# Softplus by one ScalarE activation function in a fused attention and MLP kernel

## The chip, the cores and the metric

One Trainium2 chip, one of its cores. The metric is the device time of one execution in microseconds (us). The kernel before has a median of 710.45 us over three runs (707.38 to 711.43).

The engines go by the names of the profile: PE is TensorE (matmuls) and PEld its weight loads, DVE is VectorE, ACT is ScalarE, POOL is GpSimd, SP is the engine whose queue issues the transfers. Each engine runs its own instructions in a fixed order and waits where a result of another engine is missing.

## What is computed

Eight batches of eight heads. Attention runs both ways between 512 rows of `x` and 32 rows of `state` per head; the 544 result rows of a batch then go through a two-layer network with softplus between the layers (4,352 rows, 512 to 2048 to 512).

```python
scores = scale * x @ state.T;  a = softmax(scores);  xread = a @ state
scores2 = scale * state @ x.T; a2 = softmax(scores2); sread = a2 @ x
rows = concat([xread, sread])          # per batch: 512 + 32 rows, heads side by side
h = rows @ w_in
g = np.maximum(h, 0.0) + np.log1p(np.exp(-np.abs(h)))
out = g @ w_out
```

## The kernel before

All operands are float32. For the large products every operand is split into a high part, rounded to the type `fp32r` (line 90 on ACT, or line 83 on POOL), and a low part, the remainder (line 91 on DVE or POOL); a product is then three passes: high by high, low by high, high by low. The attention result and the first layer are merged: `state @ w_in` is formed once for the heads (tiles `Vf`, split into `vhl`), so the hidden layer of a batch is attention weights `aT` times `vhl`.

The unit of work is one hidden tile of 128 features by 512 rows. `gemm1` (line 478) writes it into a PSUM bank `h`, of which there are two. `softplus` (lines 460 to 469) turns it into `ghi` and `glo`, of which there are three each, and `gemm2` (line 485) multiplies them into four accumulators `acc`. Each bank `h` is given back when the last instruction that reads it is done: line 465 on DVE, which reads it for the maximum. There are 136 such tiles, 16 for each of the eight batches and 8 for the `sread` rows of all batches (line 525 in place of line 478). A queue `pend` puts `gemm2` of a tile about three tiles behind its `gemm1`.

Strings of letters set the program order: `|` is a `gemm1` with its softplus, `g` a `gemm2`, `p` the split of a piece of `vhl`, `F` a fetch, `W` the preparation of a tile of `w_out`, `v`, `V`, `U` pieces of `state @ w_in`, and `a`, `b`, `c` the next step of the attention of a batch. `START` runs while the weights arrive, then `BLOCK2`, `BLOCK3` and `BLOCK` for the batches 2 to 6, then the `sread` tiles and `LAST`. From this program order the framework makes the order of each engine, by dependences and its own durations.

What else ACT does matters here. In `START` it converts the 64-bit weights (`as_f32`, line 111, an activation called Prelu), copies `state @ w_in` out of PSUM (lines 165, 172, 207, 216) and saves partial sums (line 574). Through all batches it makes the softmax exponentials (line 361 for `a`, line 380 for `a2`: `e2`, which PE transposes at line 392), copies PSUM (lines 240, 351, 395, 422), and rounds high parts (line 90). ACT evaluates functions from a table that holds one set of functions; line 50 loads the set `natural_log_exp_and_others` once at the start, and the instruction that does it is ACT_TABLE_LOAD. The program is compiled with such a load wherever a function is called that the loaded set lacks.

Of the kernel before, what the change touches and what calls it, by code (L numbers as in the profile page):

```python
# [13 lines left out]
AF = mybir.ActivationFunctionType  # L14
ALU = mybir.AluOpType
# [32 lines left out]
def attention_then_softplus_mlp(ctx: ExitStack, tc, xn, xt, zq, zp, stk, w_in, w_out, out):  # L48
    nc = tc.nc
# [8 lines left out]
    def sb(tag, shape, dt=F32, bufs=1):  # L58
        uid[0] += 1
        return sp.tile(shape, dt, tag=tag, name=f"{tag}_{uid[0]}", bufs=bufs)  # L60
# [25 lines left out]
    def split(hi, lo, src, *what):  # L86
        if ("hi",) + what in MOVED:
            pool_copy(hi, src)
        else:
            nc.scalar.copy(hi, src)  # L90
        vec(*what).tensor_tensor(lo, src, f32(hi), ALU.subtract)  # L91
# [367 lines left out]

    def softplus(h, *what):  # L460
        t = sb("t", [P, 512], bufs=2)
        nc.scalar.activation(t, h, AF.Abs)  # L462
        nc.scalar.activation(t, t, AF.Exp, scale=-1.0)  # L463
        nc.scalar.activation(t, t, AF.Ln, bias=1.0)  # L464
        nc.vector.scalar_tensor_tensor(t, h, 0.0, t, ALU.max, ALU.add)  # L465
        ghi = sb("ghi", [P, 512], F32R, bufs=3)
        glo = sb("glo", [P, 512], F32R, bufs=3)
        split(ghi, glo, t, "g", *what)
        return ghi, glo

    def gemm1(b, ft):
        h = bank("h", 2)
        n = 0
        cs = slice(P * (ft % 2), P * (ft % 2) + P)
        assert made["aT", b] == 2
        for g in range(2):
            for vi, ai in PASSES:
                nc.tensor.matmul(h, Vhl[b, ft // 2][:, vi, g, cs], aT[b][:, ai, g], start=(n == 0), stop=(n == 5))  # L478
                n += 1
        return softplus(h, min(b, 4), ft)  # L480
# [37 lines left out]
    def gemm1_read(u):  # L518
        assert made["read"] == B
        h = bank("h", 2)  # L520
        for i in range(2):
            n = 0
            for kt in range(4):
                for wi, si in PASSES:
                    nc.tensor.matmul(h[:, 256 * i:256 * i + 256], Whl[u, i][:, wi, kt, :], sreadT[:, si, kt, :],  # L525
                                     start=(n == 0), stop=(n == 11))
                    n += 1
        return softplus(h, B, u)
# [186 lines left out]
```

## Time and profile before

| | before |
|---|---|
| median of three runs | 710.45 us |
| profiled execution, its own time | 708.3 us |
| its span, first to last instruction | 706.3 us |
| PE busy | 680.7 us (96%) |
| ACT busy | 501.3 us (71%) |
| DVE busy | 466.3 us (66%) |
| POOL busy | 172.8 us (24%) |
| mean granted TensorE clock | 0.995 |

The span is told from the first to the last instruction; 2.0 us of the profiled execution's time lie around it. "Busy" is the share of time in which an engine has an instruction in execution. An instruction of ACT starts before the one ahead of it is quite finished, when it doesn't depend on it, so the distance between two starts is a little shorter than the duration of one. A wait is told by the engine that stood still, the line it stood at and the instruction that ended the wait. A granted clock of 1.00 is TensorE's upper level (2.4 GHz), 0.50 its lower one (1.2 GHz).

### The profile page before, as it was taken

To read this page: it belongs to the slowest core of one execution; us is meant where nothing else is said; L and a number is where in the kernel's file an instruction comes from. 1 tells how busy PE (TensorE), PEld (TensorE's weight loads), DVE (VectorE), ACT (ScalarE), POOL (GpSimd) and SP (SyncE) were. 2 spreads that over 40 slices of the span, in tenths; PEclk is the share of its full clock that TensorE was granted. 3 is DMA by queue.
4 is the path that set the end of the run, shared out by engine and by line. 5 is a ranking of instruction groups with operands and counts; after the bars stand their busy time and mean duration, and the time that the engine had idled before them with its cause. 6 is when DMAs were issued, how large, how long until landed. Compare 5 with 4: busy or idle time off the path is not lost.

```text
span 706.3 us, 9196 instructions
## 1 busy us (share of the span) xinstructions
PE 680.7 (96%) x3012; PEld 536.0 (76%) x3012; DVE 466.3 (66%) x818; ACT 501.3 (71%) x914; POOL 172.8 (24%) x170
## 2 busy tenths in 40 slices
PE   5679999999999999999999999999999999999997
PEld 2455666888877878778777887888788888888876
DVE  4499768936798997796858754875487534544322
ACT  2588988766588778799878856875687556657452
POOL 1221102665233565201201070107010510000220
PEclk9999999999999999999999999999999999999999
DMA  8768896221335456354433311320111013412001
GB/s 267 239 246 287 265 306 199 74 61 48 96 104 164 149 162 204 105 198 153 132 92 108 103 52 38 104 75 14 47 60 59 5 58 104 143 52 60 1 0 59
DMA packets 42063, 82.91 MB, mean 117 GB/s; under 512 B 6176, under 2 KB 13088, under 8 KB 42016
## 3 DMA queue, kind: packets, MB, share of 16 engines
q1 hardware_dynamic: 42016, 82.33, 36.3%
q8 instruction: 23, 0.38, 0.2%
q14 instruction: 24, 0.20, 0.1%
HBM read 56.62 MB, written 25.69 MB: 117 GB/s over the span
## 4 chain that ended last, share of the span: by engine, by line
PE 81%; ACT 9%; DVE 7%; issue 2%; DMA 1%; POOL 0%; SPq 0%; ACTq 0%; DVEq 0%; POOLq 0%
PE acc L485 47%; PE h L478 22%; PE h L525 3%; PE aux L235 2%; PE aux L411 1%; ACT t L463 1%; ACT t L462 1%; ACT t L464 1%; ACT ghi L90 1%; PE aux L341 1%; PE aux L347 1%; DVE k L91 1%; PE aux L392 1%; DMA xT<-in_xt_dram 1%; PE aux L200 1%
## 5 line engine op out<-in xcount | busy, mean ns | idle before, releaser
L485 PE MATMUL acc<-wout,ghi 128*128 128x512 f32 x1088 | 343.1, 394 | 0.9 <-DVE StK L577 0.5
L485 PEld LDWEIGHTS acc<-wout,ghi 128*128 128x128 f32 x1088 | 203.2, 188 | 48.2 <-issue 2.4
L485 PE MATMUL acc<-wout,glo 128*128 128x512 f32 x544 | 214.1, 394 | 0.0
L478 PE MATMUL h<-aT,vhl 128*128 128x512 f32 x768 | 203.7, 402 | 4.3 <-DVE t L465 3.8
L478 PEld LDWEIGHTS h<-aT,vhl 128*128 128x128 f32 x768 | 142.2, 189 | 44.4 <-DVE t L465 9.6
L465 DVE SCALAR_TENSOR_TENSOR t<-h,t 128x512 f32<-128x512 f32 x136 | 93.1, 686 | 97.4 <-ACT t L464 97.1
L462 ACT ACTIVATE t<-h 128x512 f32<-128x512 f32 x136 | 81.4, 598 | 77.4 <-DVE glo L91 37.7
L485 PEld LDWEIGHTS acc<-wout,glo 128*128 128x128 f32 x544 | 102.1, 188 | 22.7 <-issue 0.7
L91 DVE TENSOR_TENSOR glo<-t,ghi 128x512 fp32r<-128x512 f32 x100 | 70.3, 703 | 35.4 <-ACT ghi L90 14.8
L90 ACT CAST ghi<-t 128x512 fp32r<-128x512 f32 x104 | 64.5, 620 | 36.4 <-PE acc L485 23.2
L464 ACT ACTIVATE t<-t 128x512 f32<-128x512 f32 x136 | 86.2, 634 | 2.8
L463 ACT ACTIVATE t<-t 128x512 f32<-128x512 f32 x136 | 86.3, 634 | 2.2
L91 DVE TENSOR_TENSOR vhl<-vf,vhl 128x512 fp32r<-128x512 f32 x62 | 47.1, 760 | 36.0 <-ACT vhl L90 34.0
L83 POOL TENSOR_SCALAR ghi<-t 128x512 fp32r<-128x512 f32 x32 | 21.7, 679 | 180.7 <-PE acc L485 139.8
L91 POOL TENSOR_TENSOR glo<-t,ghi 128x512 fp32r<-128x512 f32 x36 | 48.5, 1351 | 49.6 <-ACT ghi L90 43.1
L90 ACT CAST vhl<-vf 128x512 fp32r<-128x512 f32 x59 | 36.4, 616 | 18.1 <-PE h L525 11.7
L368 POOL TENSOR_TENSOR T<-T,sm 128x512 f32<-128x512 f32 x13 | 15.1, 1160 | 120.7 <-DVE sm L367 92.3
L111 ACT ACTIVATE k<-k 128x512 f32<-128x512 f32 (+1 forms) x32 | 20.2, 645 | 10.3 <-DMA k<-in_w_in_dram 7.7
L525 PEld LDWEIGHTS h<-sreadT,vhl 128*128 128x128 f32 x192 | 23.6, 191 | 2.4 <-DVE t L465 2.2
L525 PE MATMUL h<-sreadT,vhl 128*128 128x256 f32 x192 | 24.9, 286 | 0.1
L352 DVE TENSOR_TENSOR k<-aux,k 64x512 f32<-64x512 f32 x24 | 16.4, 682 | 12.5 <-ACT k L351 12.3
L115 DVE SCALAR_TENSOR_TENSOR wt<-k,wt 128x512 int32<-128x512 int32 (+1 forms) x26 | 20.2, 791 | 2.0 <-ACT k L111 1.7
(161 smaller groups left out, 697.6 us busy)
## 6 DMA issues: line engine op xcount, KB each, us to landing
vd<-ve SPq DMA_DIRECT2D x44, 256.0 KB, 3.0
xT<-in_xt_dram SPq DMA_DIRECT2D x16, 512.0 KB, 4.1
x<-in_xn_dram SPq DMA_DIRECT2D x16, 512.0 KB, 3.8
k<-in_w_out_dram SPq DMA_DIRECT2D x16, 512.0 KB, 4.8
vf<-vd SPq DMA_DIRECT2D x64, 128.0 KB, 2.6
k<-in_w_in_dram SPq DMA_DIRECT2D x12, 512.0 KB, 4.7
out_dram<-o SPq DMA_DIRECT2D x24, 256.0 KB, 2.0
wt<-wsc SPq DMA_DIRECT2D x16, 256.0 KB, 2.9
```

The lines of the kernel that those rows point to most:

```text
L83: nc.gpsimd.tensor_scalar(dst, src, 1.0, 0.0, ALU.mult, ALU.add)
L90: nc.scalar.copy(hi, src)
L91: vec(*what).tensor_tensor(lo, src, f32(hi), ALU.subtract)
L111: nc.scalar.activation(h2, f32(hi), AF.Prelu, scale=2.0 ** -112, alpha=-(2.0 ** 32))
L115: nc.vector.scalar_tensor_tensor(u, h2.bitcast(I32), 3, u, ALU.logical_shift_left, ALU.bitwise_or)
L462: nc.scalar.activation(t, h, AF.Abs)
L463: nc.scalar.activation(t, t, AF.Exp, scale=-1.0)
L464: nc.scalar.activation(t, t, AF.Ln, bias=1.0)
L465: nc.vector.scalar_tensor_tensor(t, h, 0.0, t, ALU.max, ALU.add)
L478: nc.tensor.matmul(h, Vhl[b, ft // 2][:, vi, g, cs], aT[b][:, ai, g], start=(n == 0), stop=(n == 5))
L485: nc.tensor.matmul(acc[c], g[gi][:, c0:c0 + P], wout[ft][:, wi], start=(ft == first and i == 0), stop=(ft == last and i == 2))
L525: nc.tensor.matmul(h[:, 256 * i:256 * i + 256], Whl[u, i][:, wi, kt, :], sreadT[:, si, kt, :], start=(n == 0), stop=(n == 11))
```

## The change

The softplus of a tile is one activation instead of three and a DVE instruction. The reading of `h` on DVE is gone, and with it the four instructions' intermediate values in `t`. Strings, tiles and numbers of buffers stay as they are. Behind the changed lines all line numbers fall by three (line 574 becomes 571).

```diff
     def softplus(h, *what):
         t = sb("t", [P, 512], bufs=2)
-        nc.scalar.activation(t, h, AF.Abs)
-        nc.scalar.activation(t, t, AF.Exp, scale=-1.0)
-        nc.scalar.activation(t, t, AF.Ln, bias=1.0)
-        nc.vector.scalar_tensor_tensor(t, h, 0.0, t, ALU.max, ALU.add)
+        nc.scalar.activation(t, h, AF.Softplus)
         ghi = sb("ghi", [P, 512], F32R, bufs=3)
```

The order of ACT at the first softplus of the program, before. `t` is the softplus tile, `h` its bank, `k` the words of a weight tile (line 111), `T` the softmax of `a`.

```order
L111 ACTIVATE k_69_272<-k_64_261 128x512
L462 ACTIVATE t_364<-h_357 128x512
L90 CAST sreadT<-h_344 64x2x32
L463 ACTIVATE t_364<-t_364 128x512
L464 ACTIVATE t_364<-t_364 128x512
L90 CAST sreadT<-h_344 64x2x32
L361 ACTIVATE T_375<-T_375 128x512
L111 ACTIVATE k_86_321<-k_76_290 128x512
L111 ACTIVATE k_88_328<-o_108 128x256
```

The same place after the change.

```order
L111 ACTIVATE k_69_272<-k_64_261 128x512
L462 ACT_TABLE_LOAD
L462 ACTIVATE t_364<-h_357 128x512
L90 CAST sreadT<-h_344 64x2x32
L90 CAST ghi_366<-t_364 128x512
L111 ACT_TABLE_LOAD
L111 ACTIVATE k_86_321<-k_76_290 128x512
L111 ACTIVATE k_88_328<-o_108 128x256
```

Two activations of `t` are gone, the rounding of `ghi` stands where they stood, and the table is loaded twice: once for the softplus and once for the next weight conversion. The second place is ACT in the attention of a later batch, at the exponential of `a2` (line 380), before.

```order
L462 ACTIVATE t_3610<-h_3603 128x512
L380 ACTIVATE e_890_3704,rs_3705<-k_883_3671,nm_3701 128x512
L463 ACTIVATE t_3610<-t_3610 128x512
L464 ACTIVATE t_3610<-t_3610 128x512
L90 CAST a2T_3720<-aux_3715 128x8x64
L90 CAST ghi_3599<-t_3594 128x512
L361 ACTIVATE T_3723<-T_3723 128x512
L462 ACTIVATE t_3634<-h_3627 128x512
```

The same exponentials after the change.

```order
L380 ACT_TABLE_LOAD
L380 ACTIVATE e_890_3500,rs_3501<-k_883_3467,nm_3497 128x512
L462 ACT_TABLE_LOAD
L462 ACTIVATE t_3415<-h_3408 128x512
L90 CAST ghi_3404<-t_3402 128x512
L90 CAST a2T_3516<-aux_3511 128x8x64
L361 ACT_TABLE_LOAD
L361 ACTIVATE T_3519<-T_3519 128x512
L90 CAST ghi_3417<-t_3415 128x512
L462 ACT_TABLE_LOAD
L462 ACTIVATE t_3436<-h_3429 128x512
```

Four loads stand around the two exponentials; the casts and copies between them need none. In all there are 60 loads in the changed program where one was. Of the 59 new ones 24 stand from the first softplus to the last weight conversion, all in `START`, one before the softplus that follows it, and 34 in the rest, before exponentials of the attention and the softplus behind them. The order on PE and DVE is shifted by a few places in `START` too, since the framework places instructions by when it takes their inputs to be there.

## Rows read from the trace of the kernel before

**Rows 1.** The page, first part: busy time, share of the span and number of instructions of each engine.

```profile
PE 680.7 (96%) x3012; PEld 536.0 (76%) x3012; DVE 466.3 (66%) x818; ACT 501.3 (71%) x914; POOL 172.8 (24%) x170
```

**Rows 2.** Busy time in five stretches of the span: start and end, length, then busy us and number of instructions of PE, PEld, DVE, ACT and POOL, the granted clock, the DMA engines' busy share and GB/s.

```profile
0.00:35.60 35.60, 22.32 (x66) 13.23 (x67) 15.15 (x40) 14.53 (x34) 6.94 (x12) 0.95 0.76 255
35.60:42.00 6.40, 3.17 (x11) 2.22 (x10) 6.03 (x16) 5.65 (x14) 2.27 (x2) 0.86 0.65 264
42.00:95.00 53.00, 51.00 (x189) 33.91 (x188) 45.80 (x85) 48.90 (x94) 7.33 (x8) 0.98 0.83 270
95.00:132.00 37.00, 36.74 (x141) 25.69 (x140) 29.60 (x48) 31.15 (x62) 9.49 (x8) 1.00 0.64 208
132.00:706.30 574.30, 567.46 (x2612) 460.91 (x2610) 369.69 (x633) 401.11 (x716) 146.79 (x141) 1.00 0.28 87
```

**Rows 3.** Groups of instructions by line: the four instructions of a softplus and the table load at the start. Behind the bar stand busy us in total and mean ns of one; behind the second bar the idle time of the engine just before them.

```profile
L463 ACT ACTIVATE t<-t 128x512 f32<-128x512 f32 x136 | 86.3, 634 | 2.2
L464 ACT ACTIVATE t<-t 128x512 f32<-128x512 f32 x136 | 86.2, 634 | 2.8
L462 ACT ACTIVATE t<-h 128x512 f32<-128x512 f32 x136 | 81.4, 598 | 77.4 <-DVE glo L91 37.7 <-PE h L478 30.7 <-POOL glo L91 8.4
L465 DVE SCALAR_TENSOR_TENSOR t<-h,t 128x512 f32<-128x512 f32 x136 | 93.1, 686 | 97.4 <-ACT t L464 97.1
L50 ACT ACT_TABLE_LOAD x1 | 1.3, 1283 | 0.7 <-PEq L696 0.7
```

**Rows 4.** ACT in order of time, 85.0 to 92.5 us: start, duration (us), line, operation, tiles. No row has an idle time in brackets, so ACT waited for nothing here.

```profile
85.58 0.60 ACT L462 ACTIVATE t<-h 128x512 f32<-128x512 f32 x1
86.08 0.61 ACT L90 CAST ghi<-t 128x512 fp32r<-128x512 f32 x1
86.58 0.64 ACT L463 ACTIVATE t<-t 128x512 f32<-128x512 f32 x1
87.12 0.57 ACT L207 COPY wout<-aux 64x512 f32<-64x512 f32 x1
87.59 0.64 ACT L464 ACTIVATE t<-t 128x512 f32<-128x512 f32 x1
88.25 0.59 ACT L207 COPY wout<-aux 64x512 f32<-64x512 f32 x1
...
90.34 0.64 ACT L463 ACTIVATE t<-t 128x512 f32<-128x512 f32 x1
90.87 0.68 ACT L111 ACTIVATE k<-k 128x512 f32<-128x512 f32 x1
91.44 0.63 ACT L464 ACTIVATE t<-t 128x512 f32<-128x512 f32 x1
91.97 0.48 ACT L419 ACTIVATE sr<-aux,rs 128x256 f32<-128x256 f32 x1
```

**Rows 5.** All engines in order of time around the first softplus and the second (start, duration, engine, line, operation; idle time before in brackets).

```profile
36.92 0.60 ACT L462 ACTIVATE t<-h 128x512 f32<-128x512 f32 x1 [0.62 <-PE h L478]
...
39.37 0.69 DVE L465 SCALAR_TENSOR_TENSOR t<-h,t 128x512 f32<-128x512 f32 x1
...
40.11 2.84 PE L478 MATMUL h<-aT,vhl 128*128 128x512 f32 x6 [3.23 <-DVE t L465]
...
41.84 0.69 DVE L91 TENSOR_TENSOR glo<-t,ghi 128x512 fp32r<-128x512 f32 x1
...
43.88 0.81 PE L485 MATMUL acc<-wout,ghi 128*128 128x512 f32 x2
...
52.72 0.68 DVE L91 TENSOR_TENSOR glo<-t,ghi 128x512 fp32r<-128x512 f32 x1
...
58.07 0.62 PE L485 MATMUL acc<-wout,ghi 128*128 128x512 f32 x2
```

**Rows 6.** Waits in the stretch 132 to 706.3 us, of PEld and of PE (engine, line, what ended the wait: us in total, times, longest).

```profile
PEld h L478 <- DVE t L465: 4.9, 13, 0.5
PEld aux L392 <- ACT e L380: 2.5, 8, 0.6
PEld aux L411 <- DVE a2T L91: 2.3, 3, 1.7
PEld h L525 <- DVE t L465: 2.2, 6, 0.5
...
PE aux L411 <- DVE a2T L91: 1.2, 1, 1.2
...
PE aux L392 <- ACT e L380: 0.2, 1, 0.2
```

**Rows 7.** Groups by line: the exponentials of the attention on ACT, in the later batches and for `a`.

```profile
L361 ACT ACTIVATE T<-T 128x512 f32<-128x512 f32 x16 | 10.1, 628 | 5.3 <-DVE T L360 3.6 <-POOL T L360 1.7
L380 ACT ACTIVATE e<-k,nm 128x512 f32<-128x512 f32 x12 | 8.6, 716 | 1.6 <-DVE nm L377 1.6
```

## The prediction, made before the changed kernel was run

> **What bounds the kernel now.** I read the busy shares first, then the stretches, then the softplus instructions, then the waits of PE. Over the whole span PE is busy 680.7 of 706.3 us [rows 1], so nearly all of the time is matmul time and no change to ACT or DVE can win more than a few per cent. What can be won or lost lies in where PE is not busy, and in whether something else gets slower than PE. The stretches tell two stages apart [rows 2]. From 132 us on PE is busy 567.46 of 574.3 us, ACT 401.11 and DVE 369.69: there PE alone is the limit. From 42 to 95 us PE is busy 51.0 of 53.0 us and ACT 48.9 of 53.0, with short gaps between instructions that make up the rest; in that stage of weight preparation ACT stands beside PE as a second limit, and DVE with 45.8 is not far. From 95 to 132 us ACT is busy 31.15 of 37. Anything added to ACT is thus paid in one stage and hidden in the other.
>
> **What the change removes.** For each of the 136 tiles two activations go, of 634 ns each, and one DVE instruction of 686 ns; the remaining activation reads the same bank and shape as the one of 598 ns that it replaces, and I cost it the same, because the three functions before and the weight conversion all lie between 598 and 680 ns for this shape [rows 3, 4]. On ACT an activation that stands between others takes less than its duration from the queue: the starts of rows at 86.58 and 87.12, 87.59 and 88.25, 90.34 and 90.87, 91.44 and 91.97 are 0.53 to 0.66 apart [rows 4]. Their mean is (0.54 + 0.66 + 0.53 + 0.53) / 4 = 0.57 us, so a tile gives ACT back 1.14 us, 155 us over the program. DVE gets back 93.1 us [rows 3]. Both are worth time only where ACT or DVE holds up PE.
>
> **What it adds.** 59 table loads. The one load in the trace took 1283 ns [rows 3]. It stands at the start with nothing around it, so the trace doesn't show what a load costs between activations. From below I take 1.28 us. From above the nearest thing is the overlap that two neighbours lose: durations of 0.64 against distances of 0.53 to 0.54 [rows 4] mean some 0.1 us on each side, so 1.48 us, and that is the value I use, as an estimate. The load is of the engine itself, which runs in order, so behind it in ACT's queue wait the softplus or conversion it was placed for and all casts and copies after that; who waits for these is PE, for free banks and split operands.
>
> The page "ScalarE: Activation LUTs" of the Trainium skill (section "What ACT_TABLE_LOAD costs") gives about 1283 ns for the load, as the row here has it, and a DRAIN of about 1380 ns more, 2.66 us for a switch; its rule is to batch activations by set, which speaks against this change. The page "ScalarE activation tables: per-element evaluation and per-set limits" (section "What a function is on this engine") counts 1283 ns alone. No row here shows a switch in the middle of work, so the first of these is a rival below.
>
> **The stage of weight preparation.** I sum ACT's queue from the first softplus, which starts at 36.92 us [rows 5], to two places that both orders share. To the multiplication of line 419 at 91.97 us [rows 4] nine softplus run in either order, and 13 new loads lie between (the first load stands ahead of the first softplus, where ACT was idle 0.62 us [rows 5]). Gone: 18 x 0.57 = 10.3 us. Added: 13 x 1.48 = 19.2 us. Net +8.9 us, or 13 x 1.28 - 10.3 = +6.3 at the lower price. To the end of the partial sums' copies of the second turn, near 132 us, 16 softplus and 22 loads: 22 x 1.48 - 32 x 0.57 = 32.6 - 18.2 = +14.4 us, or +9.9 at the lower price. Against this stands what ACT had to spare from 95 to 132 us, 37.0 - 31.15 = 5.9 us [rows 2]: 14.4 - 5.9 = 8.5, about what the first place gave. So ACT comes out of this stage some 8.7 us late.
>
> PE does not feel all of that, because ACT works ahead of it. The low part of the first tile started on DVE at 41.84 us and its first `gemm2` at 43.88, 2.0 us later; for the second tile it is 52.72 and 58.07, 5.4 us later [rows 5]. About 3 us of lead can be eaten before PE stands still. PE has next to no idle time of its own in which to catch up later (51.0 of 53.0 us busy here, 567.46 of 574.3 behind [rows 2]), so what remains is lost for good: 8.7 - 3 = 5.7, say +6 us. Bounds: at the lower price with the larger lead, 6.3 - 5.4, about +1 us; with all of 14.4 felt, +14 us.
>
> The first visible wait goes, but I don't add it as a gain. PE stood 3.23 us until line 465 gave back the first bank [rows 5]; with a load at 36.3 us and a softplus behind it the bank is free near 38.3, 1.8 us sooner. What follows is limited by ACT's queue, in which these microseconds are already counted.
>
> **The batches behind it.** From 132 us on 120 tiles give ACT back 120 x 1.14 = 137 us, and 35 loads take 35 x 1.48 = 52. ACT has more time than before, so as a sum nothing is lost; only single waits count. PEld stood 4.9 us for a bank given back by line 465, and 2.2 us at line 525 [rows 6]; a bank is now free after one activation instead of three and a DVE instruction, even with a load ahead. Those are waits of the weight loads, part of which the running matmul covers, so I take 3 of the 7.1 us. Against this, each exponential of `a2` has a load in front. The transposes of line 392 waited 2.5 us for them, eight times [rows 6]. There are 12 in the later batches [rows 7]; where ACT arrives early the load runs while it would have waited, and ACT is now early more often. If all 12 came late by a full load it would be 12 x 1.28 = 15 us; I take one in ten, 1.5 us. Net -1.5 us, bounds -6 (all 7.1 won, little lost) and +6. DVE's relief hides under PE here and is costed at nothing.
>
> **Sum.** 708.3 + 6 - 1.5 = 712.8 us against the profiled execution's own time. The median of the runs shown is 2.15 us above that execution; on its scale the forecast is 715. I give 714, between the two, some 0.5% over the median. That is near the limit: about 0.5%, 3.6 us, is what a measurement of this kernel can tell from no change.
>
> **Rivals.**
> First, faster: ACT's lead is larger than I think and the latency of a softplus is what counts. For it: PE was busy 51.0 of 53.0 us in the very stage in which ACT had no idle time [rows 2], so PE was hardly starved; and both banks come free sooner. The stage then costs nothing, the first wait gives back 1.8 us, and the later waits 3 to 6: 708.3 - 1.8 - 3.5 = 703 us. Against it: ACT's queue is 6 to 9 us longer at a place that PE must pass. It decides by whether the lead is above some 8 us.
>
> Second, no change: the lead covers the shortage up to a few us, and the gain of later batches takes back the rest: 708 to 709 us, on the median's scale 710.
>
> Third, much slower: a switch of tables also waits until ACT is empty, before and behind. If a load between two activations waited for a full activation on each side, it would cost 0.63 + 1.28 + 0.63 = 2.54 us [rows 3, 4]; to the end of the stage that is 22 x 2.54 - 18.2 = 37.7 us, less 5.9 to spare and 3 of lead +29, and the time 737 us. For it: the only load in the trace has no activation beside it, so nothing excludes it. Against it: neighbours on ACT that depend on each other already start when the one ahead ends, without a gap of that size [rows 4]. By the page's 2.66 us, named above, it would be 22 x 2.66 - 18.2 - 8.9 = +31, or 739 us.
>
> Fourth, that the change doesn't shorten the softplus: if the one activation took as long as the three, ACT would be 32 x 0.57 = 18.2 us later in the stage, 708.3 + 6 + 18 = 732. All functions in the rows have one duration for this shape, so I give it 2 in 100.
>
> **How the numbers follow.** Forecast 0.45, faster rival 0.20, no change 0.20, drain 0.13, longer activation 0.02. The forecast's own spread, 709 to 722, lies for a quarter within 0.5%. Faster by over 0.5%: 0.20. Within: 0.20 + 0.11 = 0.31. Slower: 0.34 + 0.13 + 0.02 = 0.49. For 8 in 10 the range takes in the faster rival and the forecast's upper bound, and reaches halfway to the drain: 703 to 730 us.
>
> **What would show it.** ACT's loads should read 1.28 us, with the start of the next activation right behind, and no separate wait. From 42 to 95 us the changed trace should show ACT without idle time and PE below 51 of 53, with waits of PE and PEld ended by ACT (conversions, copies, `ghi`); the copies of line 571 (574 before), which ended near 132 us, should end some 6 us later. From there to the end the span should be as long as before or a little shorter, with no wait of line 478 for a softplus. I am wrong if PE's busy share in the first 132 us rises, if loads show 2.5 us and more between neighbours, or if the transposes of line 392 wait over 5 us in total.

## The result and the profile after

| | before | after |
|---|---|---|
| median, 10 runs each | 708.56 us (705.79 to 711.43) | 714.52 us (712.06 to 717.77) |
| profiled execution, its own time | 708.3 us | 712.73 us |
| its span | 706.3 us | 709.8 us |

The changed kernel is slower: the ratio of the times is 1.0083, with a 95% interval of 1.0058 to 1.0107, some 6 us. The forecast was 714.

The two profiled executions differ by less, 4.4 us, and their spans by 3.5. The reason lies ahead of the change. PE starts its first `gemm1` at 35.25 us before and at 32.70 after, though the matmuls up to there are the same and no changed instruction has run. The granted clock of the first 35.6 us was 0.95 before and 1.00 after; eight matmuls of line 405 took 3.68 us there before and 1.99 after. So this execution of the kernel after had a head start of 2.55 us, and 3.5 + 2.55 is the 6 us of the medians. In the traces of the experiments the first `gemm1` starts between 32.58 and 38.91 us. Times in `START` are therefore compared below from a kernel's own first `gemm1` or first softplus.

The first part of the page of the kernel after answers to [rows 1]: ACT lost 78 us of busy time and DVE 82, and the kernel still takes longer.

```profile
PE 678.6 (96%) x3012; PEld 534.1 (75%) x3012; DVE 384.2 (54%) x682; ACT 423.5 (60%) x701; POOL 172.9 (24%) x170
```

The same five stretches as in [rows 2], of the kernel after: start and end, length, then busy us and instructions of PE, PEld, DVE, ACT and POOL, granted clock, DMA share, GB/s.

```profile
0.00:35.60 35.60, 20.84 (x70) 12.13 (x70) 17.70 (x47) 17.03 (x38) 7.50 (x13) 1.00 0.80 270
35.60:42.00 6.40, 4.12 (x13) 3.10 (x14) 5.92 (x14) 6.21 (x15) 1.76 (x2) 0.86 0.70 280
42.00:95.00 53.00, 48.50 (x175) 31.26 (x174) 34.71 (x68) 51.52 (x80) 7.18 (x7) 0.99 0.70 236
95.00:132.00 37.00, 35.41 (x136) 24.59 (x135) 24.22 (x40) 35.17 (x55) 7.90 (x7) 1.00 0.74 238
132.00:709.80 577.80, 569.72 (x2622) 462.98 (x2620) 301.63 (x516) 313.62 (x518) 148.53 (x142) 1.00 0.28 87
```

From 42 to 95 us ACT now works 51.52 of 53 us, while DVE fell from 45.80 to 34.71; ACT alone stands beside PE. For what PE lost, the 97 us from its first `gemm1` on are compared, before and after, since in the first 35.6 us it was also busy longer for less at the lower clock (22.32 us for 66 matmuls, against 20.84 for 70):

```profile
35.25:132.25 97.00, 91.51 (x342) 62.34 (x341) 82.03 (x147) 86.01 (x167) 19.35 (x19) 0.98 0.74 245
32.70:129.70 97.00, 87.38 (x321) 58.12 (x320) 67.55 (x127) 93.21 (x148) 16.03 (x16) 0.98 0.74 251
```

PE did 4.1 us less, and the clock is no part of that: its mean was granted at 0.98 in both, close to the upper level.

Where PE stood still from 42 to 95 us in the kernel after (engine, line, what ended the wait: us in total, times, longest). ACT ended all of it:

```profile
PE h L475 <- ACT t L462: 1.8, 1, 1.8
PE h L475 <- ACT aT L90: 1.1, 1, 1.1
PE aux L392 <- ACT wout L207: 0.6, 1, 0.6
PE aux L167 <- ACT vf L165: 0.3, 1, 0.3
PE aux L200 <- ACT ve L216: 0.3, 1, 0.3
PE aux L405 <- ACT a2T L395: 0.2, 1, 0.2
```

The sum is 4.3 us. The same view of the kernel before sums to 1.9, mostly ended by DVE:

```profile
PE aux L200 <- DVE wout L115: 0.9, 1, 0.9
PE h L478 <- DVE t L465: 0.5, 1, 0.5
PE aux L211 <- ACT a2T L395: 0.3, 1, 0.3
PE acc L485 <- ACT StK L574: 0.2, 1, 0.2
```

The longest of the waits after, seen on ACT in order of time (start, duration, line, operation, tiles):

```profile
72.40 1.16 ACT L207 COPY wout<-aux 64x512 f32<-64x512 f32 x2
73.46 0.62 ACT L90 CAST wout<-wt 128x512 fp32r<-128x512 f32 x1
74.10 1.28 ACT L462 ACT_TABLE_LOAD   x1
75.39 0.60 ACT L462 ACTIVATE t<-h 128x512 f32<-128x512 f32 x1
```

and on PE (the idle time before the row, and what ended it, in brackets):

```profile
73.61 0.66 PE L392 MATMUL aux<-ident,e 128*128 128x128 f32 x4 [0.65 <-ACT wout L207]
76.04 0.97 PE L475 MATMUL h<-aT,vhl 128*128 128x512 f32 x3 [1.77 <-ACT t L462]
```

The copy of line 207 is late, then the load stands between the cast and the softplus, and PE waits 1.77 us for the bank; 1.28 of these are the load's duration. The wait is put down to the softplus, and the instruction ahead of it on ACT is the cause.

Groups by line of the kernel after, which answer to [rows 3]: the softplus and the loads by the line that they stand ahead of.

```profile
L462 ACT ACTIVATE t<-h 128x512 f32<-128x512 f32 x136 | 81.1, 599 | 93.2 <-PE h L475 46.3 <-DVE glo L91 36.9 <-POOL glo L91 8.6
L462 ACT ACT_TABLE_LOAD x30 | 38.5, 1283 | 3.9 <-PE h L475 3.4
L111 ACT ACT_TABLE_LOAD x11 | 14.1, 1283 | 0.2
L361 ACT ACT_TABLE_LOAD x9 | 11.5, 1283 | 0.2
L380 ACT ACT_TABLE_LOAD x9 | 11.5, 1283 | 0.2
```

The one activation takes 599 ns where line 462 took 598. The later batches, which answer to [rows 6], in the waits of PEld from 132 us to the end, after:

```profile
PEld h L475 <- ACT t L462: 6.6, 18, 0.7
PEld h L522 <- ACT t L462: 4.4, 8, 0.9
PEld aux L448 <- issue: 1.8, 5, 0.4
PEld aux L411 <- DVE a2T L91: 1.7, 2, 0.9
PEld aux L392 <- ACT e L380: 1.7, 5, 0.4
```

The waits for a bank are 11.0 us where they were 7.1, and PE itself is idle for 8.1 us from 132 us to the end (577.80 less 569.72) where it was 6.8. Shorter softplus, longer waits: that was not foreseen, and the experiments had to explain it.

### The profile page after: what moved, and what is told of

It reads as the page before. It is cut to its first block, busy times and chain, and to the rows that moved or that the text cites. A ratio compares the mean times of both kernels' runs of the same rounds, so it can differ in the third digit from the quotient of the medians.

```text
span 709.8 us, 8853 instructions
## 1 busy us (share of the span) xinstructions
PE 678.6 (96%) x3012; PEld 534.1 (75%) x3012; DVE 384.2 (54%) x682; ACT 423.5 (60%) x701; POOL 172.9 (24%) x170
## 4 chain that ended last, share of the span: by engine, by line
PE 75%; ACT 9%; DVE 7%; DMA 5%; issue 3%; SPq 1%; POOL 1%; DVEq 0%; ACTq 0%; POOLq 0%
PE acc L482 44%; PE h L475 20%; PE h L522 4%; DMA k<-in_w_in_dram 2%; PE aux L235 2%; ACT t L462 2%; PE aux L411 1%; DMA vf<-vd 1%; DVE glo L91 1%; PE aux L347 1%; DMA QZ<-in_zq_dram 1%; ACT k L111 1%; ACT ghi L90 1%; DMA vd<-ve 1%; PE aux L200 1%
## 5 line engine op out<-in xcount | busy, mean ns | idle before, releaser
L475 PE MATMUL h<-aT,vhl 128*128 128x512 f32 x768 | 200.6, 398 | 5.1 <-ACT t L462 3.7
L91 DVE TENSOR_TENSOR glo<-t,ghi 128x512 fp32r<-128x512 f32 x100 | 71.9, 719 | 123.2 <-ACT ghi L90 65.0
L91 DVE TENSOR_TENSOR vhl<-vf,vhl 128x512 fp32r<-128x512 f32 x62 | 45.0, 726 | 89.2 <-ACT vhl L90 79.8
L462 ACT ACT_TABLE_LOAD x30 | 38.5, 1283 | 3.9 <-PE h L475 3.4
L250 DVE TENSOR_TENSOR R<-wt,R 64x512 fp32r<-64x512 f32 x24 | 18.4, 768 | 6.9 <-ACT R L249 3.8
L235 PE MATMUL aux<-R,StK 128*128 128x512 f32 x64 | 20.0, 401 | 0.1
```

What stands on the lines that cost most here:

```text
L235: nc.tensor.matmul(pb, StK[i][:, h, :], r, start=(i == 0), stop=(i == 1))
L250: vec("R", *what, o).tensor_tensor(r[z], wf[a], f32(r[a]), ALU.subtract)
L462: nc.scalar.activation(t, h, AF.Softplus)
```

## The experiments

The experiments come in three groups, each compared with runs of the kernel before on the same chip. Line numbers of the experiments are shifted by a few lines. The table has all of them; the last column is PE's busy time in the 97 us from its first `gemm1` on, in the profiled execution (91.5 before): how much of its work PE did while the weights were prepared. The mean granted clock of these 97 us is 0.98 or 1.00 in every row.

| kernel | buffers of `t` | loads | median, us | ratio and interval | PE busy in 97 us |
|---|---|---|---|---|---|
| the change | 2 | 60, everywhere | 714.52 | 1.0083 [1.0058, 1.0107] | 87.4 |
| e1 no softplus | 2 | 1 | 720.42 | 1.0154 [1.0132, 1.0177] | 89.6 |
| e2 softplus in START | 2 | 31 | 724.34 | 1.0214 [1.0190, 1.0237] | 86.4 |
| e3 softplus behind START | 2 | 32 | 711.42 | 1.0024 [1.0008, 1.0041] | 89.1 |
| e4 no Prelu | 2 | 44 | 720.48 | 1.0148 [1.0127, 1.0170] | 85.5 |
| e5 no softplus | 3 | 1 | 705.42 | 0.9972 [0.9950, 0.9994] | 91.8 |
| e6 the change | 3 | 60, everywhere | 712.06 | 1.0057 [1.0029, 1.0085] | 86.2 |
| e7 before | 3 | 1 | 706.84 | 0.9988 [0.9973, 1.0004] | 91.6 |
| e8 three activations in START | 2 | 32 | 707.64 | 1.0005 [0.9989, 1.0021] | 91.5 |
| e9 softplus in START | 3 | 31 | 712.43 | 1.0061 [1.0036, 1.0086] | 87.3 |
| e10 softplus behind START | 3 | 32 | 705.52 | 0.9963 [0.9944, 0.9982] | 91.0 |
| e11 three activations in START | 3 | 32 | 704.18 | 0.9947 [0.9929, 0.9966] | 91.6 |
| e12 no Prelu | 3 | 44 | 712.78 | 1.0064 [1.0041, 1.0088] | 86.3 |

**First group: are the loads the cause, and which?** The function is replaced by Relu, which needs no load here, in all tiles (e1), behind the first 32 (e2), or in the first 32 (e3).

```diff
-        nc.scalar.activation(t, h, AF.Softplus)
+        nc.scalar.activation(t, h, AF.Relu)
```

```diff
+        nc.scalar.activation(t, h, AF.Softplus if tile_no[0] <= 32 else AF.Relu)
```

```diff
+        nc.scalar.activation(t, h, AF.Relu if tile_no[0] <= 32 else AF.Softplus)
```

e1, no loads:

> Every softplus is one activation of the set that is loaded anyway (Relu, so the output is not the softplus): one activation per tile as in the change, and 1 table load in the program instead of 60. My theory (the loads in the stage of weight preparation make ACT late, and PE pays): the time falls by 8 to 12 us against the change, to 702 to 707 us. Rival (the moved order on PE and DVE is what costs): it stays at 711 us or more, since this kernel's order is moved as well. Rival (loads in the later batches): also 702 to 707, told apart by the next two.

e2, loads in START alone:

> Softplus for the first 32 tiles, Relu for the 104 tiles behind them (their part of the output is not the softplus): 29 new loads, 25 of them in the stage of weight preparation, and hardly any behind it. My theory: 711 to 715 us, about the change's time, with the stretch to 135 us as long as in the change. Rival (later loads): 702 to 707 us, as without loads.

e3, loads behind START alone:

> The reverse: Relu for the first 32 tiles (not the softplus there), Softplus for the other 104: 31 new loads, all behind the stage of weight preparation, around the attention's exponentials. My theory: within 2 us of the kernel without loads, 703 to 708 us. Rival (later loads): 709 to 714 us.

Without any load the kernel is not faster but slower still, 1.0154. The theory that the loads are the whole cost fell. Yet the four kernels with two buffers add up: the loads in START cost 1.0214 - 1.0154 = 0.60% where the later tiles have none, and 1.0083 - 1.0024 = 0.59% where they have theirs. The loads behind START go with 1.3% less time in both pairs (1.0024 against 1.0154, 1.0083 against 1.0214). Something else is wrong, worst where ACT is fastest: in the later batches, and by the last column some 2 us in `START` of e1 and e3 too (89.6 and 89.1 against 91.5 before). A place in e1 shows it (all engines in order of time; start, duration, engine, line, idle time before):

```profile
527.17 1.45 DVE L91 TENSOR_TENSOR glo<-t,ghi 128x512 fp32r<-128x512 f32 x1
...
528.66 0.60 ACT L462 ACTIVATE t<-h 128x512 f32<-128x512 f32 x1 [1.52 <-DVE glo L91]
529.31 1.23 PEld L475 LDWEIGHTS h<-aT,vhl 128*128 128x128 f32 x6 [1.20 <-ACT t L462]
529.31 1.65 PE L475 MATMUL h<-aT,vhl 128*128 128x512 f32 x6 [0.78 <-ACT t L462]
```

The softplus waits at the head of ACT's queue, and not for its bank `h`: it waits for `t`. There are two buffers of `t`, and the one that it wants is read by `glo` of two tiles earlier. `glo` comes after `ghi`, and `ghi` has three buffers that `gemm2` gives back. So by the program the softplus cannot start before PE has got far enough with `gemm2`, PE cannot go on without the bank that this softplus holds, and everything behind it on ACT waits too. The place shows the wait for `glo` and PE's wait behind it; the way from `gemm2` to `ghi` is read off the program and off the sum of the waits (of the 98.4 us for which ACT stood before `ghi` in e1, `gemm2` ended 97.2). At this place `glo` itself took 1.45 us, where 0.7 is usual.

e4 takes away the weight conversion's need of a table instead: Prelu becomes a scaled copy and an instruction more on DVE.

```diff
-        nc.scalar.activation(h2, f32(hi), AF.Prelu, scale=2.0 ** -112, alpha=-(2.0 ** 32))
+        nc.scalar.activation(h2, f32(hi), AF.Copy, scale=-(2.0 ** -80))
+        nc.vector.scalar_tensor_tensor(h2, f32(hi), 2.0 ** -112, h2, ALU.mult, ALU.max)
```

> The change, with the weight conversion of line 111 no longer by Prelu: a scaled copy, which every set has, and one more DVE instruction (scale and maximum) for each of the 32 weight tiles. 43 loads instead of 59 new ones, those around the conversions gone. My theory: ACT loses about 16 loads of 1.4 us, 22 us, in the stage that limits, and DVE has room for 24 times 0.7 = 17 us there; 705 to 709 us. Rival (order, or later loads): 712 us or more. If DVE becomes the limit in that stage: 710 to 716 us.

It took 720.48 us, slower than the change, and PE did least of all kernels in those 97 us. Nine loads are left in `START`, around the softplus and the exponentials of the attention. It is taken up again as e12.

**Second group: a third buffer for `t`.** The memory comes from a constant tile that now shares a buffer.

```diff
-    Z4 = cp.tile([P, 4, P], F32, name="Z4")
+    Z4 = sb("zhl", [P, 4, P], bufs=2)
...
-        t = sb("t", [P, 512], bufs=2)
+        t = sb("t", [P, 512], bufs=3)
```

e5, no loads (Relu, as e1) with three buffers:

> The kernel without loads (Relu in place of the softplus), with a third buffer for t; the memory comes from putting the zero-padded state tile into a buffer of another tag that is free until the third batch. First theory (loads cost) fell with the runs before. New theory, the ring: softplus k must wait until the low part of tile k-2 has been read out of t, that waits for ghi, and ghi for the gemm2 of tile k-3, while the bank h, and all that stands behind it on ACT, waits for the softplus; the shifted order runs PE into it. It says that the third buffer takes back most of the loss: 704 to 711 us instead of 720. Rival (the order alone, whatever the buffers): 717 us or more.

e6, the change with three buffers:

> The change with the third buffer for t. Ring theory: the stage of the sread tiles gives back 2 to 3 us, so 710 to 712 us, and less if the ring also costs something in the stage of weight preparation. Rival (loads in the stage of weight preparation alone): 714 us as before, since ACT's sum there is the same. Rival (order alone): 714 +- 4.

e7, the kernel before with three buffers, a control:

> The kernel before with the third buffer: the control. Ring theory: its bank is given back by DVE after three activations and its order has PE come later, so it gains little: 706 to 710 us. If the third buffer helps every version alike, it gains as much as the change does, 704 to 706 us.

The kernel without loads falls from 1.0154 to 0.9972, some 13 us, by the buffer alone. The kernel before doesn't feel it (0.9988, the interval includes 1). The groups of the softplus by line show what went. In e1 and in e5 (behind the second bar the idle time of ACT before it, and what ended it):

```profile
L462 ACT ACTIVATE t<-h 128x512 f32<-128x512 f32 x136 | 81.1, 598 | 125.5 <-PE h L475 59.1 <-DVE glo L91 51.8 <-POOL glo L91 13.1
```

```profile
L462 ACT ACTIVATE t<-h 128x512 f32<-128x512 f32 x136 | 81.3, 598 | 114.6 <-PE h L475 85.3 <-DVE glo L91 28.0 <-POOL aT L83 0.7
```

Waits that `glo` ended fell from 64.9 to 28.0 us; the softplus now waits mainly for its own input. PEld's waits for a bank, from 132 us to the end, are two lines in e1 and one in e5:

```profile
PEld h L475 <- ACT t L462: 11.1, 19, 1.6
PEld h L522 <- ACT t L462: 4.4, 8, 0.9
```

```profile
PEld h L475 <- ACT t L462: 1.6, 4, 0.4
```

From 15.5 to 1.6 us: so the waits of e1 were those for the buffer of `t`. In e6 the waits of PEld from 132 us to the end shrink as well, from the 11.0 us of the change:

```profile
PEld h L475 <- ACT t L462: 2.5, 7, 0.4
PEld aux L392 <- ACT e L380: 2.0, 6, 0.4
```

At line 522 there is no such wait left. But e6 as a whole is at 1.0057, and its interval overlaps that of the change: the buffer is at most a small part of its loss. Whether the loads are the rest is asked in e8 and the third group.

e8 puts the three activations and the DVE instruction back for the first 32 tiles, with two buffers:

```diff
+        if tile_no[0] > 32:
             nc.scalar.activation(t, h, AF.Softplus)
+        else:
+            nc.scalar.activation(t, h, AF.Abs)
+            nc.scalar.activation(t, t, AF.Exp, scale=-1.0)
+            nc.scalar.activation(t, t, AF.Ln, bias=1.0)
+            nc.vector.scalar_tensor_tensor(t, h, 0.0, t, ALU.max, ALU.add)
```

> Three activations and the maximum for the first 32 tiles, one Softplus for the other 104: ACT and DVE work as before in the stage of weight preparation, 31 loads behind it. If half of the loss arises in the stage of weight preparation and half at the sread tiles: 710 to 712 us. If it all arises behind: 714 us. If it all arises in the first stage: 707 to 709 us.

1.0005 [0.9989, 1.0021]: without loads in START nothing is lost, and nothing won either; PE's 97 us are those of the kernel before (91.5). This run splits the result by the prediction's own terms: START cost 1.0083 - 1.0005 = 0.78% or 5.5 us (some 2 us either way, from the two intervals), the later batches 0.05%, 0.4 us (-0.8 to +1.5).

**Third group: all with three buffers.** e9, softplus in START alone (as e2):

> Three buffers for t; Softplus in the first 32 tiles, Relu in place of it in the 104 behind (those tiles are left without the softplus), so nearly all loads stand in START. Theory (with the third buffer the loads of START alone cost the time): about as the change with three buffers, ratio 1.004 to 1.007, 710 to 713 us. Rival (the loads before the exponentials of the later batches cost it): as the kernel without loads and three buffers, ratio 0.996 to 0.999, about 705 us.

e10, softplus behind START alone (as e3):

> Three buffers for t; Relu in place of the softplus in the first 32 tiles (left without it), Softplus in the 104 behind, so the loads stand in the later batches. Theory (START's loads cost): ratio 0.996 to 0.999, 704 to 707 us, like the kernel without loads and three buffers. Rival (the later loads cost): ratio 1.004 to 1.007, 710 to 713 us.

Both came out as the theory said and against the rival. Loads in START cost 1.0061 - 0.9972 = 0.89% with no loads behind, 1.0057 - 0.9963 = 0.94% with them: 6.3 and 6.7 us. Loads behind START cost nothing that these runs can tell, some 2 us either way: 0.9963 against 0.9972, 1.0057 against 1.0061. So the 1.3% by which they seemed to help with two buffers belonged to the buffers.

e11, as e8 with the third buffer:

> Three buffers for t; the first 32 tiles with the three activations and the DVE instruction of before, Softplus behind. Theory (no loads in START, later batches gain some 3 us, and the third buffer takes back the 2.4 us of the sread tiles): ratio 0.994 to 0.998, 704 to 707 us, faster than before. Rival (the loss at the sread tiles has another cause than the buffer): no better than the same kernel with two buffers, ratio 1.000, 707 to 709 us.

704.18 us, 0.9947 [0.9929, 0.9966]: the fastest of all, 0.5% under the kernel before, with no part of the computation left out. PE's 97 us from the first `gemm1` are as before (91.6), and the waits for a bank behind it are those of e6 and not those of the change (PEld, 132 us to the end; line 484 is `gemm1`, line 466 the softplus):

```profile
PEld aux L392 <- ACT e L380: 2.6, 7, 0.6
PEld h L484 <- ACT t L466: 2.4, 7, 0.4
```

e12, as e4 with the third buffer:

> Three buffers for t; the weight conversion's Prelu replaced by a scaled copy on ACT, which needs no load, and an instruction more on DVE. If the loads of START and the buffer were all that the two-buffer form of this lost: ratio 0.996 to 1.002, 705 to 710 us. If DVE in START, which gets an instruction for each conversion, is what limits it: ratio over 1.007, 713 us and more.

1.0064, between the two expectations and above the first, so the buffer was a part of e4's loss and not all of it. Its stretches from 42 to 132 us:

```profile
42.00:95.00 53.00, 47.30 (x168) 30.54 (x168) 47.59 (x93) 49.30 (x84) 7.94 (x7) 0.97 0.74 245
95.00:132.00 37.00, 34.16 (x129) 23.25 (x128) 30.98 (x53) 22.67 (x44) 5.48 (x5) 1.00 0.70 231
```

DVE has 78.6 of these 90 us, against 58.9 in the kernel after, and PE is as short of work as with the loads. That DVE's queue is the cause is argued from these rows; no run separates it from the longer way of each piece from ACT to DVE and back, nor from the nine loads that are left in START of e12 (all before 95 us, where the kernel after has 14).

## Why the prediction was right, and where not

**The forecast as a whole** was a little nearer in the number than in the change. It added 4.5 us to the profiled execution; the medians differ by 6.0. That 714 and 714.52 lie so close is in part luck: the scale of 715 rested on a median of three runs, 710.45, and with ten runs it is 708.56. The rival of no change is out by the interval.

**The price of a load** was right. A load ends 1.28 us after its start and the activation behind it starts at once: 74.10 and 75.39. Ahead of it the overlap is lost, 0.64 us from the cast at 73.46 to the load, where neighbours were 0.53 apart [rows 4]. Together that is 1.40 us of ACT's queue a load; 1.48 was assumed. The other loads are alike: each starts within 0.03 us of the end of the instruction or the wait ahead of it. The drain rival is thereby out. The Trainium skill, page "ScalarE: Activation LUTs", section "What ACT_TABLE_LOAD costs", has a DRAIN of about 1380 ns beside the load for every switch to a different set; the trace disagrees, since 0.02 us between the cast's end and the load, and 1.29 us from the load's start to the next activation, leave no room for it. The rival of a longer activation is out by 599 ns.

**The +6 us in START** was right in size: 5.5 us by e8, 6.3 and 6.7 us by e9 and e10. Its working was not, at two steps that nearly cancelled, and that is luck. "ACT comes out of this stage some 8.7 us late" was too much. The stretch is from the first softplus, at 36.92 us before [rows 5], to the multiplication of line 419, at 91.97 [rows 4]; in ACT's timeline of the kernel after these are

```profile
35.06 0.60 ACT L462 ACTIVATE t<-h 128x512 f32<-128x512 f32 x1
...
95.40 0.46 ACT L419 ACTIVATE sr<-aux,rs 128x256 f32<-128x256 f32 x1
```

It took 60.34 us where it had taken 55.05: 5.3 more, not 8.9. Between the two stand the nine softplus and 13 loads that the prediction counted. At 1.40 us a load instead of 1.48 the sum is 13 x 1.40 - 10.3 = 7.9. The rest is idle time: ACT stood still in this stretch for 3.4 us before (4.0 in the view from 36.92, less the 0.62 ahead of the softplus itself) and for 0.7 after, so 2.7 us of it took up the longer queue, and 7.9 - 2.7 = 5.2. The two largest sums of these waits, before:

```profile
ACT aT L90 <- DVE k L371: 1.7, 1, 1.7
ACT t L462 <- PE h L478: 1.3, 2, 0.6
```

The prediction had read what ACT was not busy in this stage as "short gaps between instructions", and so had given it no spare time. "About 3 us of lead can be eaten before PE stands still" was too much as well. In the 59.75 us from its first `gemm1` PE had done 2.8 us less than before (51.72 against 54.52), and after 97 us 4.1 less, which leaves some 1.2 of ACT's 5.3. ACT does many things besides `ghi` for PE, and the waits of 42 to 95 us are for a bank, for `aT`, for copies of lines 207, 165, 216 and 395; a lead read off the `glo` of two tiles says nothing of those. The copies of line 571 were to end some 6 us later; the last starts 101.0 us after PE's first `gemm1`, against 96.8 for line 574, so 4.3 us later.

**The -1.5 us of the later batches** measured +0.4 us (-0.8 to +1.5) in e8, so the term's sign isn't shown, and its reasons failed. "A bank is now free after one activation instead of three and a DVE instruction" holds only for a softplus that may start. The prediction had looked at who reads the bank and not at who still reads the tile that the softplus writes: no wait of line 478 for a softplus was expected, and 6.6 us of them came, with 4.4 at line 522. That the three activations and the instruction on DVE hid it before is argued from e7, where the third buffer changes nothing. With the third buffer the gain exists: from e7 to e11 it is 0.9988 to 0.9947, 0.4% or 2.9 us (some 1.7 us either way), about what "I take 3 of the 7.1 us" had hoped for. The loads ahead of line 380 cost less than the 1.5 us assumed: line 392 waited 1.7 us for `e` where it had waited 2.5 [rows 6], and e9 against e6 shows nothing lost for 29 more loads.

**The faster rival** rested on the latency of a softplus. Its first step was real: PE's first wait for a bank, 3.23 us [rows 5], became 1.37 (PE in order of time, after):

```profile
35.71 1.64 PE L475 MATMUL h<-aT,vhl 128*128 128x512 f32 x6 [1.37 <-ACT t L462]
```

But a short softplus in START wins nothing even where it brings no loads: e3 and e10, with Relu there, are not faster than e8 and e11 with all three activations (1.0024 against 1.0005, where the two buffers cost e3 some 2 us in START; 0.9963 against 0.9947). Time given back to ACT in START was worth nothing; time added to it cost 5.5 to 6.7 us.

**What stays open.** The framework places instructions by its own durations, so each kernel here has an order of its own: in START, ACT and DVE run in another order in e5 than in e6, which differ in the function alone. That START costs what it does by the loads, and not by the order that comes with them, is therefore argued from ACT's queue, whose sum closes (5.2 against 5.3 us), and not separated by a run. That the third buffer makes a kernel with the single activation faster is shown in five pairs (e1 and e5, e2 and e9, e3 and e10, e4 and e12, e8 and e11); between the change and e6 the intervals overlap. Whether e1 lost more than e3 because no loads slowed the softplus down, or because its order ran into the buffer more often, was not separated. Nor was the remaining loss of e12.

## What to carry to other kernels

Count table loads by stage: the 30 of e9, 23 of them in the first 132 us, where ScalarE has next to no spare time, cost some 6 us, and the 31 of e10 behind it, under a TensorE that is the limit alone, cost nothing that could be told; so a function with a set of its own is used only there (e11). The Trainium skill has a rule to batch activations by set (page "ScalarE: Activation LUTs", section "Table sets: the hidden batching unit"); by these runs it had something to save in that stage and next to nothing in the rest, though no run here batched them. Before two traces are compared by their times, look whether they come to the first changed instruction at the same time: here 2.55 us lay ahead of it, by a lower clock. When a step is made shorter, look at every buffer that it writes as well as at what it reads, since the next limit may be a ring of buffers that the longer step had hidden; one buffer more was worth 13 us without loads.

## What was not expected of the hardware

A load between activations took some 1.40 us of ACT's queue and no more: 1283 ns in each of the 60 places, with the next activation 1.29 to 1.36 us behind its start in 58 of the 59 new ones (in the other it waited for DVE). Nothing else in the runs was unexpected of the hardware; what surprised, the wait for a buffer of `t`, is the kernel's own.
